# A SwiGLU feed-forward layer: part of the down projection split into two 64-row halves by tile position

## The chip, the core and the metric

The kernel runs on one core of a Trainium2 chip. A core has TensorE (PE in the profile: matrix products, with its weight loads shown apart as PEld), VectorE (DVE), ScalarE (ACT), GpSimd (POOL) and SyncE (SP), which issues transfers. The engines run their own instruction streams and wait for one another by semaphores. TensorE reads its operands from SBUF and writes sums to PSUM, which has eight banks of 512 f32 values per partition; ACT and VectorE read PSUM and write back to SBUF, and DMA moves SBUF to and from device memory. The metric is the device time of one execution in microseconds (us), taken as the median of several runs.

## The reference

```python
B, S, D, F = 1, 2048, 640, 1536        # all bfloat16
def reference(x, w_gate, w_up, w_down):
    g = silu(x @ w_gate)
    u = x @ w_up
    return (g * u) @ w_down
```

`x` is 2048 rows of 640 numbers; the hidden size F is 1536. The two projections up take 2 x 2048 x 640 x 1536 multiplications, the projection down half as many as those two together.

## The kernel before, in words

Everything on chip is kept transposed, with the contracted dimension on the partitions: `xT` (x with D on partitions, KD = 5 blocks of 128), `wg_sb` and `wu_sb` (5 blocks of 128 rows of D), `wd_sb` (KF = 12 blocks of 128 rows of F), and `aT`, the product of silu(gate) and up, with F on the partitions in 12 blocks. The rows of x are worked through in four blocks of 512 (`sb` = 0 to 3).

For each block and each of the 12 chunks of F (`fc`), `proj` (L204) runs five matmuls into a gate bank `pg` and five into an up bank `pu`; `gate` then runs silu on ACT (L221) and the multiplication into `aT` on VectorE (L222). Four PSUM banks (`gu`) rotate here. When a block's 12 chunks are done, the down projection of that block follows, in two parts:

- Columns 512 to 639 of the output, the "column-by-row" part that is edited: twelve matmuls (L287), one for each block `kf` of F, with a 128 x 128 block of `wd_sb` as the weights and 512 columns of `aT` streamed (384 in the last block, whose last 128 rows of x are done otherwise). They accumulate in one bank, `po_t`, from the pool tag `po_b`, which has two banks. The result has output columns on partitions, so it must be turned: ACT copies it to `ot_t` in bf16 (L296), VectorE turns it in squares of 32 (`ot_q`, L298), and ACT's queue issues four stores (L300).
- Columns 0 to 511: for each of the four sub-blocks of 128 rows (`j`), a chain of twelve matmuls (L316) with `aT` as the weights and 512 columns of `wd_sb` streamed, into one of the two banks of tag `po_a`. ACT copies the result (L325) and SP's queue issues the store (L334). The last sub-block of all runs as two chains of 256 columns and one of 128 (the rows that the first part left out), the last one in a bank of tag `po_b` and copied by VectorE (L328).

VectorE has a further task. The last T = 4 rows of x are left out of the `proj` matmuls of the last block, and their gate and up values are computed as dot products on VectorE (`row_dots`, L153, 96 of them, each with a short read of its accumulator). They are dealt out by `do_dots(n)`: two behind most gates, three behind the copy to `ot_t`, three behind each of `j` = 1 to 3. All of them are done before the last block's down projection; `row_tail` (L167, L168) then writes those four columns of `aT`.

The order on VectorE and on SP is the order in which the program is written (`keep_order` ties each instruction of the queue to the one before). On ACT and TensorE the instructions stand in the order written as well. Engines wait only for data and for buffers: a bank of `po_a` is free for chain j + 2 when ACT has copied chain j, and the copies stand on ACT behind the four stores of `ot_q`, which wait for the turning on VectorE.

Of the kernel before, what the change touches and what calls it, by code (L numbers as in the profile page):

```python
# [10 lines left out]
def _body(  # L11
# [8 lines left out]
    nc = tc.nc  # L20
    P = nc.NUM_PARTITIONS
    f32 = mybir.dt.float32
    bf16 = mybir.dt.bfloat16
    ACT = mybir.ActivationFunctionType
    ALU = mybir.AluOpType

    B, S0, D = x.shape
# [6 lines left out]
    KF = F // P  # L34
    S_BLK = 512
    NSB = S // S_BLK
    SUB = S_BLK // P
    DA = 512
# [13 lines left out]
    work = ctx.enter_context(tc.tile_pool(name="work", bufs=3))  # L52
    outp = ctx.enter_context(tc.tile_pool(name="outp", bufs=3))
    psum = ctx.enter_context(
        tc.tile_pool(name="psum", bufs=2, space=bass.MemoryType.PSUM)
    )
# [6 lines left out]
    wd_sb = consts.tile([P, KF, D], bf16)  # L63
    aT = consts.tile([P, KF, S], bf16)
# [45 lines left out]
    def turn_x(c0, c1, k0=0, k1=KD):  # L110
        s_sl = slice(c0 * P, c1 * P)
        nc.sync.dma_start_transpose(out=xT[:, k0:k1, s_sl], in_=xt_v[s_sl, k0:k1])
# [22 lines left out]
    def turn_w(dst, src):  # L135
        for a in range(0, KF, WT_STEP):
            nc.sync.dma_start_transpose(
                out=dst[:, a : a + WT_STEP, :], in_=src[:, a : a + WT_STEP, :]
            )
# [3 lines left out]
        out=x_row[:],  # L143
# [20 lines left out]
    def row_tail():  # L164
        for _ in dots:
            pass
        nc.scalar.activation(row_s[:], row_g[:], ACT.Silu)  # L167
        nc.vector.tensor_tensor(  # L168
            out=aT[:, :, S - T : S], in0=row_s[:], in1=row_u[:], op=ALU.mult
        )  # L170
# [3 lines left out]
    def do_dots(n):  # L174
        for _ in range(n):
            next(dots, None)
# [25 lines left out]
    def proj(ps, w_sb, fc, sb, c0, c1, k0=0, k1=KD):  # L202
        for kd in range(k0, k1):
            nc.tensor.matmul(  # L204
                ps[:, c0:c1],
                lhsT=w_sb[:, kd, fc * P : (fc + 1) * P],
                rhs=xT[:, kd, sb * S_BLK + c0 : sb * S_BLK + c1],
                start=(kd == 0),
                stop=(kd == KD - 1),
            )  # L210

    def gu_tiles():
        pg = psum.tile([P, S_BLK], f32, tag="gu", name="pg", bufs=4)
        pu = psum.tile([P, S_BLK], f32, tag="gu", name="pu", bufs=4)
        return pg, pu

    def gate(pg, pu, sb, fc, n_s):

        s0 = sb * S_BLK
        sg = work.tile([P, S_BLK], f32, name="sg")  # L220
        nc.scalar.activation(sg[:, 0:n_s], pg[:, 0:n_s], ACT.Silu)  # L221
        nc.vector.tensor_tensor(  # L222
            out=aT[:, fc, s0 : s0 + n_s], in0=sg[:, 0:n_s], in1=pu[:, 0:n_s], op=ALU.mult
        )
# [46 lines left out]
    for sb in range(NSB):  # L271
        n_s = S_BLK if sb < NSB - 1 else S_BLK - T
        for fc in range(KF):
            if sb == 0 and fc < N_FIRST:
                continue
            pg, pu = gu_tiles()
            proj(pg, wg_sb, fc, sb, 0, n_s)
            proj(pu, wu_sb, fc, sb, 0, n_s)
            gate(pg, pu, sb, fc, n_s)
            if sb > 0 and fc < KF - 2:  # L280
                do_dots(2)


        n_t = (SUB if sb < NSB - 1 else SUB - 1) * P
        po_t = psum.tile([P, n_t], f32, tag="po_b", name="po_t")
        for kf in range(KF):
            nc.tensor.matmul(  # L287
                po_t[:],
                lhsT=wd_sb[:, kf, DA:D],
                rhs=aT[:, kf, sb * S_BLK : sb * S_BLK + n_t],  # L290
                start=(kf == 0),
                stop=(kf == KF - 1),
            )
        ot_t = outp.tile([P, n_t], bf16, name="ot_t")
        ot_q = outp.tile([P, n_t], bf16, name="ot_q")
        nc.scalar.copy(ot_t[:], po_t[:])  # L296
        do_dots(3)
        nc.vector.transpose(out=ot_q[:], in_=ot_t[:])  # L298
        for q in range(P // Q):
            nc.scalar.dma_start(  # L300
                out=out2[
                    sb * S_BLK : sb * S_BLK + n_t, DA + q * Q : DA + (q + 1) * Q
                ].rearrange("(i r) c -> r i c", r=Q),
                in_=ot_q[q * Q : (q + 1) * Q, :].rearrange("r (i c) -> r i c", c=Q),
            )

        for j in range(SUB):
            s0 = sb * S_BLK + j * P
            last = sb == NSB - 1 and j == SUB - 1
            cols = [(0, DA, "po_a")]  # L310
            if last:
                cols = [(0, DA // 2, "po_a"), (DA // 2, DA, "po_a"), (DA, D, "po_b")]
            for c0, c1, tag in cols:
                po = psum.tile([P, c1 - c0], f32, tag=tag, name="po_a")
                for kf in range(KF):
                    nc.tensor.matmul(  # L316
                        po[:],
                        lhsT=aT[:, kf, s0 : s0 + P],
                        rhs=wd_sb[:, kf, c0:c1],
                        start=(kf == 0),  # L320
                        stop=(kf == KF - 1),
                    )
                ot = outp.tile([P, c1 - c0], bf16, name="ot" if c1 < D else "ot_b")
                if c1 < D:
                    nc.scalar.copy(ot[:], po[:])  # L325
                    eng = nc.sync
                else:
                    nc.vector.tensor_copy(out=ot[:], in_=po[:])  # L328
                    eng = nc.sync
                if 0 < j and not last:  # L330
                    do_dots(3)
                if sb == NSB - 1 and j == ROW_J:
                    row_tail()
                eng.dma_start(out=out2[s0 : s0 + P, c0:c1], in_=ot[:])  # L334
        if sb == 0:
            turn_x(2 * SUB, 3 * SUB)
            turn_w(wuT, wut_v)
            turn_x(3 * SUB, 4 * SUB)
# [72 lines left out]
def kernel(tc, *args):  # L411
    _body(tc, *args)
    tc.close()
    tc.compile()
    _trim(tc.nc)
# [30 lines left out]
```

## Time and profile before

| | |
|---|---|
| Time, median of 3 runs | 163.79 us (163.2 to 163.9) |
| The profiled execution | 163.25 us, of which 161.9 us are the span from the first to the last instruction |
| TensorE busy | 159.6 us, 818 matmuls, granted clock 1.000 |
| VectorE busy | 110.5 us |
| ACT busy | 42.6 us |
| The edited matmuls (L287) | 48, 6% of the chain that ended last |

An instruction is named by its line in the kernel, its engine and operation, and the tiles that it writes and reads (`po_t<-aT,wd_sb`). A group's row gives the count, the busy time in us, the mean duration of one in ns, and the engine's idle time before them with what ended it. In the view by windows of time, a row gives the stretch, its length, and for each engine its busy time in it and the instructions that touch it, then the granted clock and the transfers. A matmul's recorded duration reaches beyond the start of the next one, because matmuls are pipelined, so the pitch from start to start says what one costs in a stream. The chain that ended last lists stretches as start, length, engine and line; the timeline lists start, length and instruction, with the engine's idle time and what ended it in brackets. ACTq stands for transfers that ACT's queue issues.

### The profile page before, as it was taken

What the parts mean: (1) busy time and instruction counts of PE and PEld (TensorE: products, weight loads), DVE (VectorE), ACT (ScalarE), POOL (GpSimd) and SP (SyncE); (2) the same over time, 40 slices, a digit from 0 to 9 for tenths busy, and PEclk for the clock granted to TensorE, in tenths of its full rate; (3) what the DMA queues carried; (4) which work ended last, traced back from release to release, by engine and by line L of the source; (5) the groups of instructions that cost most, each with busy time, mean ns of one, the idle gap of its engine ahead of it and who ended that gap; (6) DMA issues with size and microseconds to landing.
All of it is one profiled execution on the core that took longest, in us unless ns stands there. A gap on an engine that the chain in (4) does not pass through costs nothing.

```text
span 161.9 us, 2159 instructions
## 1 busy us (share of the span) xinstructions
PE 159.6 (99%) x818; PEld 79.9 (49%) x818; DVE 110.5 (68%) x249; ACT 42.6 (26%) x74; POOL 0.6 (0%) x6
## 2 busy tenths in 40 slices
PE   9999999999999999999999999999999999999995
PEld 9885444444444444444444444444444444445454
DVE  1006223599469999989919999979964999993000
ACT  5032222112222222211222322221214222222121
POOL 1000000000000000000000000000000000000000
PEclk9999999999999999999999999999999999999999
DMA  7999999995089992003110000000310000000212
GB/s 228 280 345 348 363 209 241 230 190 100 32 186 139 241 225 58 0 0 34 65 65 4 0 0 2 0 0 4 64 66 32 0 0 0 0 4 0 52 37 73
DMA packets 41209, 15.86 MB, mean 98 GB/s; under 512 B 33264, under 2 KB 41072, under 8 KB 41200
## 3 DMA queue, kind: packets, MB, share of 16 engines
q1 hardware_dynamic: 32832, 14.81, 38.0%
q10 hardware_dynamic: 8368, 0.92, 3.7%
q8 instruction: 6, 0.10, 0.3%
q14 instruction: 3, 0.02, 0.1%
HBM read 6.88 MB, written 2.62 MB: 59 GB/s over the span
## 4 chain that ended last, share of the span: by engine, by line
PE 99%; DVE 0%; issue 0%
PE pu L204 32%; PE pg L204 31%; PE po_a L316 26%; PE po_t L287 6%; PE pg L250 2%; PE pw L182 1%; PE pt L195 1%; DVE ot_b L328 0%; DVE ones L108 0%
## 5 line engine op out<-in xcount | busy, mean ns | idle before, releaser
L204 PE MATMUL pu<-xT,wu_sb 128*128 128x512 bf16 (+2 forms) x260 | 59.3, 362 | 0.0
L204 PE MATMUL pg<-xT,wg_sb 128*128 128x512 bf16 (+2 forms) x240 | 56.9, 370 | 0.0
L222 DVE TENSOR_TENSOR aT<-sg,pu 128x512 bf16<-128x512 f32 (+1 forms) x48 | 32.5, 682 | 32.8 <-PE pu L204 32.8
L221 ACT ACTIVATE sg<-pg 128x512 f32<-128x512 f32 (+1 forms) x48 | 28.4, 597 | 71.1 <-PE pg L204 67.5
L316 PE MATMUL po_a<-wd_sb,aT 128*128 128x512 bf16 (+2 forms) x216 | 42.8, 358 | 0.0
L153 DVE SCALAR_TENSOR_TENSOR prod<-wgT,x_row 128x640 f32<-128x640 bf16 x48 | 39.4, 821 | 1.1
L153 DVE SCALAR_TENSOR_TENSOR prod<-wuT,x_row 128x640 f32<-128x640 bf16 x48 | 39.4, 822 | 1.0
L204 PEld LDWEIGHTS <-wu_sb 128*128 128x128 bf16 x260 | 25.4, 98 | 26.5 <-DMA wu_sb<-in_w_up_dram 0.2
L204 PEld LDWEIGHTS <-wg_sb 128*128 128x128 bf16 x240 | 23.5, 98 | 25.9
L316 PEld LDWEIGHTS <-aT 128*128 128x128 bf16 x216 | 20.7, 98 | 21.6
L325 ACT CAST ot<-po_a 128x512 bf16<-128x512 f32 (+1 forms) x17 | 9.5, 561 | 32.0 <-PE po_a L316 20.9
L287 PE MATMUL po_t<-aT,wd_sb 128*128 128x512 bf16 (+1 forms) x48 | 10.4, 366 | 0.0
L287 PEld LDWEIGHTS <-wd_sb 128*128 128x128 bf16 x48 | 4.7, 98 | 5.1
L328 DVE CAST ot_b<-po_a 128x128 bf16<-128x128 f32 x1 | 0.3, 292 | 9.9 <-PE po_a L316 9.9
L296 ACT CAST ot_t<-po_t 128x512 bf16<-128x512 f32 (+1 forms) x4 | 2.2, 559 | 11.6 <-PE po_t L287 11.6
L153 DVE DVE_READ_ACCUMULATOR prod<-wuT,x_row 128x1 f32 x48 | 4.0, 82 | 0.0
L153 DVE DVE_READ_ACCUMULATOR prod<-wgT,x_row 128x1 f32 x48 | 3.9, 82 | 0.0
L298 DVE STREAM_TRANSPOSE ot_q<-ot_t 128x512 bf16<-128x512 bf16 (+1 forms) x4 | 2.7, 678 | 1.7 <-ACT ot_t L296 1.7
L250 PE MATMUL pg<-xT,wg_sb 128*128 128x256 bf16 (+1 forms) x24 | 3.1, 307 | 0.0
L200 DVE COPY xT<-pt 128x384 bf16<-128x384 bf16 x2 | 0.7, 358 | 3.2 <-PE pt L195 3.2
L250 PEld LDWEIGHTS <-wg_sb 128*128 128x128 bf16 x24 | 2.6, 127 | 0.3
L182 PE MATMUL pw<-ones 128*128 128x128 bf16 x20 | 2.3, 313 | 0.3 <-DVE ones L108 0.3
(15 smaller groups left out, 8.0 us busy)
## 6 DMA issues: line engine op xcount, KB each, us to landing
wd_sb<-in_w_down_dram SPq DMA_DIRECT2D x1, 1920.0 KB, 14.6
out_dram<-ot SPq DMA_DIRECT2D x15, 128.0 KB, 1.7
wg_sb<-in_w_gate_dram SPq DMA_DIRECT2D x2, 640.0 KB, 6.7
wu_sb<-in_w_up_dram SPq DMA_DIRECT2D x2, 640.0 KB, 8.0
x_row<-in_x_dram SPq DMA_DIRECT2D x1, 640.0 KB, 4.9
wg_sb<-in_w_gate_dram SPq DMA_DIRECT2D x3, 128.0 KB, 3.5
wu_sb<-in_w_up_dram SPq DMA_DIRECT2D x1, 384.0 KB, 4.7
out_dram<-ot_q ACTq DMA_DIRECT2D x12, 32.0 KB, 2.1
```

The source lines that it names most:

```text
L153: nc.vector.scalar_tensor_tensor(out=prod[:], in0=wT[:, fc, :], scalar=1.0, in1=x_row[:, t, :], op0=ALU.mult, op1=ALU.mult, accum_out=acc[ ...
L182: nc.tensor.matmul(pw[:, 0:P], lhsT=ones[:].broadcast_to([P, P]), rhs=ones[:].broadcast_to([P, P]), start=True, stop=True,)
L195: nc.tensor.transpose(out=pt[:, kd - k0, :], in_=x_sb[:, c, kd * P : (kd + 1) * P], identity=ident[:],)
L204: nc.tensor.matmul(ps[:, c0:c1], lhsT=w_sb[:, kd, fc * P : (fc + 1) * P], rhs=xT[:, kd, sb * S_BLK + c0 : sb * S_BLK + c1], start=(kd == 0 ...
L221: nc.scalar.activation(sg[:, 0:n_s], pg[:, 0:n_s], ACT.Silu)
L222: nc.vector.tensor_tensor(out=aT[:, fc, s0 : s0 + n_s], in0=sg[:, 0:n_s], in1=pu[:, 0:n_s], op=ALU.mult)
L250: nc.tensor.matmul(pg[:, c0:c1], lhsT=wg_sb[:, kd, wslice(fc, fc + 1)], rhs=xT[:, kd, c0:c1], start=(kd == 0 and c0 == 0), stop=(kd == KD ...
L287: nc.tensor.matmul(po_t[:], lhsT=wd_sb[:, kf, DA:D], rhs=aT[:, kf, sb * S_BLK : sb * S_BLK + n_t], start=(kf == 0), stop=(kf == KF - 1),)
L296: nc.scalar.copy(ot_t[:], po_t[:])
L298: nc.vector.transpose(out=ot_q[:], in_=ot_t[:])
L316: nc.tensor.matmul(po[:], lhsT=aT[:, kf, s0 : s0 + P], rhs=wd_sb[:, kf, c0:c1], start=(kf == 0), stop=(kf == KF - 1),)
L325: nc.scalar.copy(ot[:], po[:])
```

## The change

The twelve matmuls of the column-by-row part become 24. Each block of 128 rows of F is cut in two halves of 64 rows: partitions 0 to 63 of `wd_sb` and `aT` go to the array at row position 0 and accumulate in the first bank, partitions 64 to 127 go to row position 64 and accumulate in a second bank. The two alternate in the program, each with a weight load of its own in front. Both banks have the tag `po_b`, so they are that tag's two buffers. At the end ACT copies the first bank to a new f32 tile `part` in SBUF, and VectorE, behind the three dot products that were there before, adds `part` and the second bank into `ot_t` in bf16. The turning and the stores follow as before. The instructions of all other engines and lines keep their places; in the whole kernel there are 48 more matmuls, 48 more weight loads and four more VectorE instructions.

```diff
         n_t = (SUB if sb < NSB - 1 else SUB - 1) * P
-        po_t = psum.tile([P, n_t], f32, tag="po_b", name="po_t")
+        half = P // 2
+        po_ts = [psum.tile([P, n_t], f32, tag="po_b", name="po_t") for _ in range(2)]
         for kf in range(KF):
-            nc.tensor.matmul(
-                po_t[:],
-                lhsT=wd_sb[:, kf, DA:D],
-                rhs=aT[:, kf, sb * S_BLK : sb * S_BLK + n_t],
-                start=(kf == 0),
-                stop=(kf == KF - 1),
-            )
+            for h, po_t in enumerate(po_ts):
+                h_sl = slice(h * half, (h + 1) * half)
+                nc.tensor.matmul(
+                    po_t[:],
+                    lhsT=wd_sb[h_sl, kf, DA:D],
+                    rhs=aT[h_sl, kf, sb * S_BLK : sb * S_BLK + n_t],
+                    start=(kf == 0),
+                    stop=(kf == KF - 1),
+                    tile_position=(h * half, 0),
+                )
         ot_t = outp.tile([P, n_t], bf16, name="ot_t")
         ot_q = outp.tile([P, n_t], bf16, name="ot_q")
-        nc.scalar.copy(ot_t[:], po_t[:])
+        part = work.tile([P, n_t], f32, name="part")
+        nc.scalar.copy(part[:], po_ts[0][:])
         do_dots(3)
+        nc.vector.tensor_tensor(
+            out=ot_t[:], in0=part[:], in1=po_ts[1][:], op=ALU.add
+        )
         nc.vector.transpose(out=ot_q[:], in_=ot_t[:])
```

## The prediction

> **What bounds the kernel now.** I read the page's busy shares and its chain that ended last first.
>
> ```profile
> PE 159.6 (99%) x818; PEld 79.9 (49%) x818; DVE 110.5 (68%) x249; ACT 42.6 (26%) x74; POOL 0.6 (0%) x6
> PEclk9999999999999999999999999999999999999999
> PE 99%; DVE 0%; issue 0%
> PE pu L204 32%; PE pg L204 31%; PE po_a L316 26%; PE po_t L287 6%; PE pg L250 2%; PE pw L182 1%; PE pt L195 1%; DVE ot_b L328 0%; DVE ones L108 0%
> ```
>
> TensorE (PE) is busy in 99% of the span at the full granted clock, and the chain is TensorE's own instructions from end to end. Whatever lengthens TensorE's stream lengthens the kernel; whatever lengthens another engine costs nothing until a buffer comes free too late for TensorE. The edited line, L287, is 6% of that chain. The chain in order of time shows its four stages and what follows each without a gap:
>
> ```profile
> 30.56 2.59 PE po_t L287 x12
> 33.15 10.36 PE po_a L316 x48
> 69.41 2.59 PE po_t L287 x12
> 72.00 10.36 PE po_a L316 x48
> 108.26 2.59 PE po_t L287 x12
> 110.85 10.36 PE po_a L316 x48
> 146.91 1.95 PE po_t L287 x12
> 148.86 11.07 PE po_a L316 x72
> ```
>
> A 512-column matmul takes 2.59/12 = 0.216 us of the stream, a 384-column one 1.95/12 = 0.162 us: the columns streamed set the pitch. The four stages hold 3 x 2.59 + 1.95 = 9.72 us. The groups with shapes kept apart, and the engines' busy time in two of those stages on that line alone:
>
> ```profile
> L287 PE MATMUL po_t<-aT,wd_sb 128*128 128x512 bf16 x36 | 8.3, 379 | 0.0
> L287 PE MATMUL po_t<-aT,wd_sb 128*128 128x384 bf16 x12 | 2.1, 326 | 0.0
> L287 PEld LDWEIGHTS <-wd_sb 128*128 128x128 bf16 x48 | 4.7, 98 | 5.1
> L316 PE MATMUL po_a<-wd_sb,aT 128*128 128x128 bf16 x12 | 0.8, 219 | 0.0
> ...
> 69.41:72.00 2.59, 2.59 (x12) 0.98 (x10) 1.00 0.00 0
> 146.91:148.86 1.95, 1.95 (x12) 0.97 (x10) 1.00 0.00 0
> ```
>
> One matmul lasts 379 ns but the next follows after 216: 163 ns of each lie under its successor (326 - 162 = 164 for the short ones). Weight loads (98 ns) lie wholly beside the matmuls.
>
> **The change, part by part.** Each of the 48 matmuls over 128 rows of f becomes two over 64 rows, at row positions 0 and 64, each with its own weight load and into its own bank. The columns streamed per instruction stay 512 or 384. So 96 matmuls and 96 loads replace 48 and 48; what decides is whether the two halves stream together.
>
> *A pair of halves.* No row shows two matmuls in the array at once. The bounds are one pitch per pair (216 and 162 ns, nothing added) and two (9.72 us more in all). Nothing in issue forbids the low end, as the end of the chain shows:
>
> ```profile
> 157.94 1.99 PE po_a L316 x24
> 159.93 0.02 issue
> 159.95 0.29 DVE ot_b L328
> ```
>
> These 24 are twelve of 256 columns, at half of 216 ns each, and twelve of 128, which leaves (1.99 - 12 x 0.108)/12 = 0.058 us for a matmul with its load. Two matmuls and two loads thus need some 0.116 us of issue, under 0.162 and 0.216. The halves share no row of the array, no bank and no operand partition. I take one pitch per pair, by reasoning and not by a row, and keep the other end as a rival. The second half's load stands in the program behind the first half's matmul, so that half trails by about 0.058 us and shows once at each stage's end: 4 x 0.058 = 0.23 us, between 0 and 4 x 0.098 = 0.39.
>
> *Entering and leaving the two-half layout.* All other matmuls use the array whole, so each of four stages changes the layout twice, eight changes. No row shows one. At the least it is free, as the step from one line's matmuls to the next is now. At the most the new layout waits until the last matmul is through (163 ns beyond its pitch) and then loads weights in the open (98 ns): 0.261 us. I take 0.163, the wait without the load, since loads run ahead beside matmuls in every row here: 8 x 0.163 = 1.30 us (0 to 2.09).
>
> The Trainium skill, "TensorEngine Tiling (Array Packing)", section Key Properties, says that a change of tiling mode drains TensorE, and that different tiles load and multiply in parallel. By the first the eight waits are there, by the second the pairs are; no row here shows either.
>
> *ACT and VectorE.* ACT's copy of the first bank has the old one's place and, into f32, still 512 columns; the row nearest to it is L221's f32 output, at 597 ns against 586, so nothing. VectorE gets four additions, one per stage, with the operands of L222's form (f32 from SBUF and f32 from PSUM, bf16 out):
>
> ```profile
> L222 DVE TENSOR_TENSOR aT<-sg,pu 128x512 bf16<-128x512 f32 x36 | 24.3, 683 | 28.4 <-PE pu L204 28.4
> L221 ACT ACTIVATE sg<-pg 128x512 f32<-128x512 f32 x36 | 21.3, 597 | 53.6 <-PE pg L204 50.1 <-DVE aT L222 3.5
> L296 ACT CAST ot_t<-po_t 128x512 bf16<-128x512 f32 x3 | 1.8, 586 | 9.2 <-PE po_t L287 9.2
> ```
>
> 0.683 us each, in front of the transpose. Behind that transpose ACT's queue holds the four `ot_q` stores and then the copy of the first `po_a` chain, which frees the bank for the third chain. In order of time (start, length), the second stage, and that copy in the other three:
>
> ```profile
> 72.03 0.59 ACT L296 CAST ot_t<-po_t 128x512 bf16<-128x512 f32 x1 [3.07 <-PE po_t L287]
> 72.65 0.71 DVE L298 STREAM_TRANSPOSE ot_q<-ot_t 128x512 bf16<-128x512 bf16 x1
> 73.39 2.07 ACTq L300 DMA_DIRECT2D out_dram<-ot_q  x4
> 75.51 0.59 ACT L325 CAST ot<-po_a 128x512 bf16<-128x512 f32 x1 [2.89 <-DMA out_dram<-ot_q]
> ...
> 36.58 0.59 ACT L325 CAST ot<-po_a 128x512 bf16<-128x512 f32 x1 [2.81 <-DVE prod L153]
> 114.28 0.59 ACT L325 CAST ot<-po_a 128x512 bf16<-128x512 f32 x1 [2.81 <-DMA out_dram<-ot_q]
> 152.00 0.59 ACT L325 CAST ot<-po_a 128x512 bf16<-128x512 f32 x1 [2.62 <-DMA out_dram<-ot_q]
> ...
> 84.62 0.69 DVE L222 TENSOR_TENSOR aT<-sg,pu 128x512 bf16<-128x512 f32 x1 [3.61 <-PE pu L204]
> ```
>
> In the second stage that copy ends at 76.10. The third chain starts two chains (2 x 2.59) after 72.00, less the 0.16 by which a matmul starts before its predecessor ends: 77.02. Slack 0.92; the other stages, reckoned alike, have 1.00, 1.00 and 1.29. An addition of 0.683 plus a hand-over of some 0.03 (72.03 + 0.59 to 72.65) leaves about 0.2 us at the tightest, more where TensorE itself is later. So I cost it at nothing; without that cover it would be up to 0.7 us in each of three stages. The next gate waits 3.61 us for TensorE on VectorE, so 0.68 more of VectorE's time is hidden there too. The stores behind the addition leave 0.7 us later in mid-kernel; SP's queue is not touched, and the `po_a` stores on it follow ACT's copy. The second bank: both `po_b` buffers are free one stage, some 36 us, before they are wanted, and in the last stage the final 128 columns take the one that ACT released ten us before. After the last matmul nothing is changed.
>
> **Sum.** 0 (pairs) + 0.23 (trail) + 1.30 (changes of layout) + 0 (ACT, VectorE) = +1.53 us, between 0 and 0.39 + 2.09 = 2.48. The profiled execution took 163.25 (span 161.9 and 1.35 around it), so 164.8; it was 0.54 under the median of the three runs, 163.79, and on that scale the forecast is 165.3.
>
> **The rivals.**
> - *Not slower: the change of layout is free.* Then only the trail remains, +0.23, 164.0 on the median's scale. For it: every step from one line to another is seamless in the chain. Against it: none of those steps changes the layout. It decides if a change costs under (0.82 - 0.23)/8 = 0.07 us, 0.82 being 0.5% of 163.79, about what a measurement of this kernel can tell from no change.
> - *The change doesn't do what it says: the halves follow one another.* 36 x 0.216 + 12 x 0.162 = 9.72 more, with the layouts 11.0: 174.8 (173.5 to 175.9). For it: every matmul in the trace starts a full pitch after the one before. Against it: disjoint rows and banks.
> - *A half's weights can't load while that half streams.* Then each pair shows a load that is covered now: 0.058 to 0.098 us x 48 = 2.8 to 4.7, with 1.30 for the layouts +4.1 to +6.0: 167.9 to 169.8. Against it: now all 128 rows stream while the next weights load, 0.98 us of loads inside 2.59 us of matmuls. The Trainium skill, "TensorE: Matmul & The Clock Gate", section Part 3 (packing small matmuls), states that LDWEIGHTS overlaps matmuls in flight only where the row group differs; by that the trace before would show gaps, and it shows none, so the trace disagrees.
> - *ACT's late copy becomes a wait.* If the addition costs double (1.37), three stages wait some 0.4 us, the last one little: about +1.3 on top, 166.6. Against it: the L222 row is the same form, 36 times.
>
> **How the numbers follow.** Pairs together with costly layout changes 0.45; pairs with free changes 0.20; halves one after another 0.20; loads exposed 0.08; ACT's wait 0.04; something faster, for which I see no mechanism, 0.03. The likeliest alone gives 165.3, with its own range 163.8 to 166.3. The other cases but the serial one hold under 0.8, so the range must reach it: 163.4 (a free change within the runs' spread of 163.2 to 163.9) to 174.8. Slower by over 0.5% means over 164.6: the serial, load and ACT cases 0.32 and all but about 0.07 of the likeliest, 0.38, so 0.70. Within 0.5%: the free change and that 0.07, so 0.27. Faster: 0.03.
>
> **What would show it.** In the profile after: L287's successor has 96 matmuls. Right: the four stages take about 2.65, 2.65, 2.65 and 2.01 us plus a wait of about 0.16 at both edges of each, with the second half starting some 0.06 after the first and pairs 0.216 apart. Serial: stages of 5.2 and 3.9. Exposed loads: pairs 0.27 to 0.31 apart. Free change: no gap at the edges. ACT's wait: TensorE idle at the third `po_a` chain, released by ACT. All else on TensorE should stand as it did; what makes the forecast wrong is the pitch of a pair first, and the price of a layout change second.

## The result, and the profile after

The changed kernel takes 164.9 us (median of five runs, 164.64 to 165.76) against 163.79 (five runs, 163.2 to 163.94): a ratio of 1.0093, 95% interval 1.0071 to 1.0115, which is 1.5 us (1.2 to 1.9); the two medians alone differ by 1.1. The profiled execution took 164.64 us with a span of 162.7.

The page of the changed kernel: the busy shares, the two groups of the halves (now L290) and the two new steps, ACT's copy to `part` and VectorE's addition.

```profile
PE 160.4 (99%) x866; PEld 79.1 (49%) x866; DVE 113.2 (70%) x253; ACT 42.6 (26%) x74; POOL 0.6 (0%) x6
...
L290 PE MATMUL po_t<-aT,wd_sb 64*128 64x512 bf16 (+1 forms) x96 | 10.4, 364 | 0.0
L290 PEld LDWEIGHTS <-wd_sb 64*128 64x128 bf16 x96 | 4.4, 94 | 5.9 <-issue 1.7
...
L301 ACT COPY part<-po_t 128x512 f32<-128x512 f32 (+1 forms) x4 | 2.2, 560 | 12.1 <-PE po_t L290 12.1
L303 DVE TENSOR_TENSOR ot_t<-part,po_t 128x512 bf16<-128x512 f32 (+1 forms) x4 | 2.6, 654 | 2.0 <-ACT part L301 1.8
```

96 matmuls in place of 48 keep TensorE busy for the same 10.4 us. The chain that ended last, in order of time, of the changed kernel:

```profile
6.61 2.36 PE pu L204 x20
...
30.60 2.70 PE po_t L290 x24
33.29 5.29 PE po_a L324 x24
39.01 5.18 PE po_a L324 x24
69.66 2.70 PE po_t L290 x24
72.36 5.29 PE po_a L324 x24
78.07 5.18 PE po_a L324 x24
108.72 2.70 PE po_t L290 x24
111.42 5.29 PE po_a L324 x24
117.14 5.18 PE po_a L324 x24
147.59 2.06 PE po_t L290 x24
149.64 11.18 PE po_a L324 x72
160.82 0.02 issue
```

A stage takes 2.70 where it took 2.59 (2.06 for 1.95), and the first 24 `po_a` matmuls behind it 5.29 where 24 pitches are 5.18 (in the last stage 11.18 for 11.07). Each of the eight layout changes thus costs 0.11 us, and behind the first stretch nothing else is longer: 8 x 0.107 = 0.86 us. The whole stream bears that out. The same row of the kernel before:

```profile
6.61 2.31 PE pu L204 x20
```

Both kernels begin the stretch of 20 `pu` matmuls at 6.61; the last matmul ended at 159.93 before and at 160.82 now, 0.89 later, of which 0.05 is that first stretch itself (2.36 for 2.31). Start to start in the trace, from the last `pu` matmul ahead of the first stage to the last matmul of all, TensorE's stream takes 129.52 us before and 130.37 now: 0.85 more.

How the halves start is seen in the view by windows, on L290 alone (length, TensorE's busy time and the instructions that touch the window, the same for weight loads), and in the waits of the weight loads:

```profile
30.52:30.54 0.01, 0.01 (x2) 0.01 (x2) 1.00 0.81 188
```

```profile
PEld L290 <- issue: 1.7, 4, 0.4
PEld L324 <- issue: 1.6, 4, 0.4
```

Within 15 ns of the start of the stage's first instruction, at 30.52, both halves are at work. (The chain counts the stage from 30.60, where the recorded end of the matmul before lies.) The start times in the trace stand 4 ns apart, and pairs follow each other after 216. The weight loads, which had no wait of this kind before, now have eight: four on entering (L290), four on leaving (L324). Such a wait of some 0.42 us counts from the end of the load before, which stands a pitch and more ahead of its time in a steady stream, so it is longer than the 0.107 us that TensorE's stream loses.

One thing in this trace the diff doesn't tell. Between the second and the third `po_a` chain of the first three stages (33.29 + 5.29 = 38.58 to 39.01) two `pg` matmuls of the next block now stand, and three follow behind the fourth chain. The planner, which lays out TensorE's order outside the parts that `keep_order` ties, moved them there. What is said ahead of the prediction, that the instructions of all other lines keep their places, is wrong in this point, and so is that TensorE's instructions all stand in the order written. Experiment 9 takes the move back.

The profiled executions differ by 1.39 us, the spans by 0.89. The other 0.50 lies outside the span, from the first to the last instruction that the trace holds: 163.25 - 161.85 = 1.40 before, 164.64 - 162.74 = 1.90 after. The prediction has no term for that; experiments 5 to 7 go after it.

### The profile page after: what moved, and what is told of

It reads as the page before. It is cut to its first block, busy times and chain, and to the rows that moved or that the text cites. A ratio compares the mean times of both kernels' runs of the same rounds, so it can differ in the third digit from the quotient of the medians.

```text
span 162.7 us, 2263 instructions
## 1 busy us (share of the span) xinstructions
PE 160.4 (99%) x866; PEld 79.1 (49%) x866; DVE 113.2 (70%) x253; ACT 42.6 (26%) x74; POOL 0.6 (0%) x6
## 4 chain that ended last, share of the span: by engine, by line
PE 95%; DMA 3%; SPq 1%; DVE 0%; issue 0%
PE pu L204 32%; PE pg L204 30%; PE po_a L324 26%; PE po_t L290 6%; DMA wu_sb<-in_w_up_dram 3%; SPq L118 1%; SPq L88 0%; DVE ot_b L336 0%
## 5 line engine op out<-in xcount | busy, mean ns | idle before, releaser
L324 PE MATMUL po_a<-wd_sb,aT 128*128 128x512 bf16 (+2 forms) x216 | 43.3, 358 | 0.0
L324 PEld LDWEIGHTS <-aT 128*128 128x128 bf16 x216 | 20.4, 98 | 22.4 <-issue 1.6
L290 PE MATMUL po_t<-aT,wd_sb 64*128 64x512 bf16 (+1 forms) x96 | 10.4, 364 | 0.0
L290 PEld LDWEIGHTS <-wd_sb 64*128 64x128 bf16 x96 | 4.4, 94 | 5.9 <-issue 1.7
L301 ACT COPY part<-po_t 128x512 f32<-128x512 f32 (+1 forms) x4 | 2.2, 560 | 12.1 <-PE po_t L290 12.1
L303 DVE TENSOR_TENSOR ot_t<-part,po_t 128x512 bf16<-128x512 f32 (+1 forms) x4 | 2.6, 654 | 2.0 <-ACT part L301 1.8
```

Of the source, the lines that this page charges most:

```text
L290: nc.tensor.matmul(po_t[:], lhsT=wd_sb[h_sl, kf, DA:D], rhs=aT[h_sl, kf, sb * S_BLK : sb * S_BLK + n_t], start=(kf == 0), stop=(kf == KF - 1),
L301: nc.scalar.copy(part[:], po_ts[0][:])
L303: nc.vector.tensor_tensor(out=ot_t[:], in0=part[:], in1=po_ts[1][:], op=ALU.add)
L324: nc.tensor.matmul(po[:], lhsT=aT[:, kf, s0 : s0 + P], rhs=wd_sb[:, kf, c0:c1], start=(kf == 0), stop=(kf == KF - 1),)
```

## The experiments

All are set against runs of the kernel before on the same chip. "Outside" is a run's time less its span, as a median; for the kernel before it was 1.38 to 1.42 in every group of runs.

**1. The price of a layout change: six times as many of them.** Only the even blocks `kf` are cut in halves.

```diff
         for kf in range(KF):
+            if kf % 2 == 1:
+                nc.tensor.matmul(po_ts[0][:], lhsT=wd_sb[:, kf, DA:D],
+                    rhs=aT[:, kf, sb * S_BLK : sb * S_BLK + n_t],
+                    start=False, stop=(kf == KF - 1))
+                continue
             for h, po_t in enumerate(po_ts):
...
-                    stop=(kf == KF - 1),
+                    stop=(h == 1 and kf == KF - 2),
```

> The changed kernel with only every other block kf cut in halves; the odd blocks run as whole matmuls into the first bank. Twelve layout changes per stage in place of two, 48 in place of 8. Theory (each change costs about 0.107 us): +5.1 us over before, 168.9; 4.3 over the changed kernel. Rival (a change costs only where a stage begins or ends, with its change of operands and banks, or the remaining 0.4 us are a cost of the pairs): 164.4 to 165.0.

Measured: 168.58 us, ratio 1.0318 (1.030 to 1.0336), 5.2 us over the 163.39 of the kernel before; 5.2/48 = 0.108 for a change. The chain of this kernel (L299 the halves, L289 the whole ones) and the loads' waits:

```profile
30.87 0.32 PE po_t L299 x2
31.19 0.32 PE po_t L289
31.52 0.32 PE po_t L299 x2
31.84 0.32 PE po_t L289
```

```profile
PEld L299 <- issue: 6.0, 24, 0.4
PEld L289 <- issue: 5.1, 24, 0.2
```

Every step between layouts is 0.32 us where the pitch is 0.216, 24 waits in and 24 out. The price is that of a change of layout as such, not of a stage's beginning.

**2. and 3. Fewer of them.** The change in the first stage only, and in the first three. The diff of the first; the other has `sb < NSB - 1`.

```diff
+        if sb == 0:
             po_ts = [psum.tile(...) for _ in range(2)]
...
+        else:
+            po_t = psum.tile([P, n_t], f32, tag="po_b", name="po_t")
...
+            nc.scalar.copy(ot_t[:], po_t[:])
```

> The change in the first of the four stages only; the other three as in the kernel before. Two layout changes in place of eight. Theory (0.107 us for each): 0.21 in TensorE's stream, span 0.2 longer than that of the kernel before. Rival (the cost is one for the whole kernel, not one for each change): 0.86 in the stream. The time outside the span: 1.7 if one addition brings it, 1.4 if not.

> The change in the first three stages; the last one as in the kernel before, so six layout changes. Theory (0.107 us for each): TensorE's stream 0.64 longer, 0.21 less than in the changed kernel. For the time outside the span: 1.75 and more in all kernels with the addition in four stages and whole or halved matmuls, 1.4 with the addition in the first stage only and in the kernels without it. If the last stage's addition (near the end of the kernel) brings it: 1.4, and 0.65 over the kernel before; if the number of additions does: 1.75, and 1.0 over.

Measured: 163.98 against 163.56, ratio 1.0026 (1.0011 to 1.0041), outside 1.38; and 164.2 against 163.44, ratio 1.0054 (1.0035 to 1.0073), outside 1.61. The loads' waits, of the kernel with one stage and of that with three:

```profile
PEld L291 <- issue: 0.4, 1, 0.4
PEld L339 <- issue: 0.4, 1, 0.4
```

```profile
PEld L339 <- issue: 1.3, 3, 0.4
PEld L291 <- issue: 1.3, 3, 0.4
```

Two waits and six. The first stage of the one reads 2.70, its other three 2.59 and 1.95: 0.21 of the 0.42 us (0.2 to 0.7) is in the stream, as the theory has it, and the interval reaches down to it. The other 0.2 lies in the span (162.6 against 162.2 by the medians) but not in the stages: in the profiled execution the last `pu` matmul ahead of the first stage starts at 30.83 where it started at 30.18 before, so the kernel's head differed, and no run says why. The three give 0.64 in the stream and 0.2 outside, 0.84 of the 0.88. One addition alone brings no time outside. Neither of the two answers offered for the time outside fits 1.61.

**4. Do the halves pair by themselves?** The loops swapped: twelve matmuls of the first half, then twelve of the second.

```diff
-        for kf in range(KF):
-            for h, po_t in enumerate(po_ts):
+        for h, po_t in enumerate(po_ts):
+            for kf in range(KF):
```

> The changed kernel with the loops swapped: all twelve matmuls of the first half, then all twelve of the second, so that neighbours in TensorE's stream use the same 64 rows. Theory (two matmuls stream together only when their row positions differ and they are neighbours in the stream): the stages double, 9.72 us more, 174.0 to 174.9, stages of 5.3 and 4.0 us. Rival (TensorE looks ahead over the stream and pairs the halves by itself, or a matmul of 64 rows costs half): as the changed kernel, 164.6 to 165.5.

Measured: 171.42 us, ratio 1.0469 (1.040 to 1.054), 7.7 us more. Both were off. The stages in this kernel's chain:

```profile
31.14 4.44 PE po_t L290 x24
...
71.95 4.44 PE po_t L290 x24
...
112.75 4.44 PE po_t L290 x24
...
153.36 3.37 PE po_t L290 x24
```

24 matmuls one after another would take 24 x 0.216 + 0.11 = 5.29. The stage is 0.85 shorter, about four pitches. Start to start, the trace shows single matmuls at 216 ns, then, with the ninth of the first half, a second one 8 ns behind it, and pairs from there until the first half is through. So TensorE started the second half's first matmul with three matmuls of the first half still in front of it in the program: matmuls of different row positions pair by neighbourhood, but over a reach of some three matmuls, not only for direct neighbours. All four stages show the same. The planner might have mixed the two lists itself; the semaphore marks in the trace speak against it. As in the kernel before, where the twelve stand alone, the tenth matmul of the first half raises TensorE's semaphore for those ahead of it, the eleventh and twelfth raise it by one each, and no matmul of the second half counts among them. A run with TensorE's order tied was not made. Two on the same 64 rows keep the full pitch, so half the rows is not half the time.

**5. The path without the halves.** Whole matmuls, the blocks alternating between two banks, with `part` and the addition.

```diff
-            for h, po_t in enumerate(po_ts):
-                h_sl = slice(h * half, (h + 1) * half)
...
+            nc.tensor.matmul(
+                po_ts[kf % 2][:],
+                lhsT=wd_sb[:, kf, DA:D],
+                rhs=aT[:, kf, sb * S_BLK : sb * S_BLK + n_t],
+                start=(kf < 2), stop=(kf >= KF - 2))
```

> The array is used whole again (12 matmuls of 128 rows per stage), but the blocks kf alternate between the two banks, and the copy to part and VectorE's addition stay. No layout change is left. Theory (the cost is eight layout changes of about 0.107 us, 0.86 us, ACT and VectorE are hidden): the time of the kernel before, 163.8 within 0.3, span 161.9. Rival (the longer path over part and the addition costs something, in the stream or behind the span): 164.3 to 164.6, the part of the 1.1 to 1.5 us that 0.86 doesn't explain.

Measured: 163.91 against 163.39, ratio 1.0026 (1.001 to 1.0042). The chain of this kernel:

```profile
69.44 2.59 PE po_t L288 x12
72.03 5.18 PE po_a L321 x24
77.21 0.43 PE pg L204 x2
77.64 5.18 PE po_a L321 x24
```

TensorE's stream is that of the kernel before to 0.01 us, so the copy, the addition and the later stores are hidden in it. But all twelve runs have 1.70 to 1.80 outside (median 1.75) against 1.38: against the kernel before on the same chip the theory's "nothing" fell by some 0.4 us, nearly all of it outside the span. That 163.91 still lies within its 163.8 +- 0.3 is chance: on this chip the kernel before took 163.39 and not 163.79.

**6. The halves without the path.** The second bank is never read.

```diff
-        part = work.tile([P, n_t], f32, name="part")
-        nc.scalar.copy(part[:], po_ts[0][:])
+        nc.scalar.copy(ot_t[:], po_ts[0][:])
         do_dots(3)
-        nc.vector.tensor_tensor(
-            out=ot_t[:], in0=part[:], in1=po_ts[1][:], op=ALU.add)
```

> The changed kernel without the second half's way out: ACT copies the first bank to ot_t in bf16 as before, and part and VectorE's addition are gone (the second half's sum is left out of the output; TensorE does all of its work). Theory (0.86 us of layout changes in the stream; the rest of the difference, 0.3 to 0.7 us, lies outside the span and goes with the addition's path): 0.9 over the kernel before, span 162.8, time outside the span 1.4 as in the kernel before. Rival (the rest goes with TensorE's matmuls by halves): 1.5 over, time outside the span 1.7 or more.

Measured: 164.64 against 163.61, ratio 1.0074 (1.0041 to 1.0107), 1.2 us (0.7 to 1.8), which holds the theory's 0.9 and the rival's 1.5; span 163.2 against 162.2 (medians); outside 1.42, with nine of twelve runs between 1.37 and 1.44 and three between 2.0 and 2.6. The stages are 2.70 and 2.06 again. The median outside is that of the kernel before, as the theory has it, but three of the twelve runs have more without any addition.

**7. What else could bring the time outside.** Three kernels: VectorE gets a tiny instruction in the addition's place; the path goes over `part`, but from one bank; and experiment 5 with a slightly longer program for TensorE.

```diff
         do_dots(3)
+        nc.vector.memset(tiny[:], 1.0)
```

> The kernel before with one tiny VectorE instruction per stage (a memset of one column, read by nobody) where the changed kernel has its addition, so four VectorE instructions more and nothing else. In the kernel with whole matmuls and the addition the stream and the span were those of before, but the time outside the span was 1.74 us against 1.38. Theory A (the time outside the span goes with the program's code, not with the work): 1.7 outside, 0.35 over the kernel before. Theory B (it goes with the path over part and the addition): 1.4 outside, no difference.

```diff
-        nc.scalar.copy(ot_t[:], po_t[:])
+        part = work.tile([P, n_t], f32, name="part")
+        nc.scalar.copy(part[:], po_t[:])
         do_dots(3)
+        nc.vector.tensor_copy(out=ot_t[:], in_=part[:])
```

> The kernel before, one bank and whole matmuls, but ACT copies the bank to part in f32 and VectorE copies part to ot_t in bf16 behind the dot products: the changed kernel's longer path without the second bank. Kernels with the addition had 1.7 us and more outside the span in four of five cases, those without it 1.4. Theory (the path, a later start of the transpose and the stores, brings it): time outside the span 1.7, 0.4 over the kernel before. Rival (it goes with the place of the program's code or with the second bank): 1.4 outside, no difference.

```diff
-    N_WARM = 20
+    N_WARM = 24
```

> The kernel with whole matmuls in two banks and the addition, with 24 in place of 20 warming matmuls at the start, so that TensorE's program is eight instructions longer and the rest the same. Theory (the time outside the span goes with the addition's path): 1.75 outside as without the four, the span longer by up to 0.4. Rival (it goes with where the program's code lies, which the four shift): another value, 1.4 or 2.1.

Measured: 163.42 against 163.61, ratio 0.9994 (0.9977 to 1.001), outside 1.42; 163.66 against 163.56, ratio 1.0008 (0.9994 to 1.0021), outside 1.39; 164.06 against 163.56, ratio 1.0031 (1.0019 to 1.0043), outside 1.76. So neither four more VectorE instructions nor the longer path from one bank brings it, and eight more instructions for TensorE don't move it. The kernels that add two banks have it: 1.75, 1.76, 1.77 (experiment 4), 1.61 with three additions, 1.94 and 2.07 in the two groups of runs of the changed kernel, 2.04 in experiment 9. Three things contradict: experiment 1 has all four additions and 1.39 outside, one addition alone gives 1.38, and three runs of experiment 6 have 2.0 to 2.6 without one. The trace holds nothing before the first and behind the last instruction, and behind the last matmul these kernels' traces are equally long (1.92 to 1.94 us, with the addition and without). What this time is stays open.

**8. More instructions without a layout change.** The matmuls of the kernel before, cut by columns.

```diff
+            for c0 in (0, n_t // 2):
+                s0 = sb * S_BLK + c0
                 nc.tensor.matmul(
-                    po_t[:],
+                    po_t[:, c0 : c0 + n_t // 2],
                     lhsT=wd_sb[:, kf, DA:D],
-                    rhs=aT[:, kf, sb * S_BLK : sb * S_BLK + n_t],
+                    rhs=aT[:, kf, s0 : s0 + n_t // 2],
```

> The kernel before with each of the 48 po_t matmuls cut into two of half the columns (256, or 192 in the last stage), whole array, one bank, no addition: as many TensorE instructions as in the changed kernel, no layout change. Theory: two halves of the columns cost one whole one, some 2 ns more each from the 109 against 108 ns pitch: +0.1 us, 163.9. Rival (48 more matmuls and weight loads cost something in themselves, by loading of code or by issue): 164.3 to 164.9.

Measured: 163.74 against 163.39, ratio 1.0021 (1.0001 to 1.0041), outside 1.42. The chain of this kernel:

```profile
30.53 2.62 PE po_t L289 x24
```

0.03 more for twelve matmuls and twelve loads more in a stage, 0.12 in all four. It is not the number of instructions that makes 2.70 out of 2.59, and the interval, 0.02 to 0.67 us, leaves the rival (0.5 to 1.1 over the 163.79 it was reckoned from) only its lower end.

**9. The moved `pg` matmuls put back.**

```diff
     keep_order(mybir.EngineType.SP)
+    keep_order(mybir.EngineType.PE)
```

> The changed kernel with TensorE's instructions held in the order of the program, so that the two pg matmuls which now stand between the second and third po_a chain go back behind the fourth. Theory (their place costs nothing; the third chain would still find its bank free about 0.3 us before it starts): the time of the changed kernel, 164.9 within 0.3, no idle TensorE at the third chain. Rival (the addition makes ACT's copy late, and the moved matmuls hide it): TensorE idle at the third chain released by ACT, 0.1 to 0.4 us in each of three stages, 165.2 to 166.1.

Measured: 165.1 us, ratio 1.0106 (1.0088 to 1.0124), which overlaps the changed kernel's interval. The chain of this kernel, and ACT's copies in its second stage:

```profile
70.16 2.70 PE po_t L290 x24
72.85 10.47 PE po_a L324 x48
```

```profile
74.97 2.09 ACTq L308 DMA_DIRECT2D out_dram<-ot_q  x4
77.10 0.59 ACT L333 CAST ot<-po_a 128x512 bf16<-128x512 f32 x1 [3.62 <-DMA out_dram<-ot_q]
```

The 48 matmuls take 10.47 where they took 10.36 before, the 0.11 of the layout change and no idle time. The third chain begins at 72.85 + 5.29 - 0.16 = 77.98, and the copy that frees its bank ends at 77.69: 0.29 us to spare, the least of the four stages, and what the theory said. TensorE's stream is the changed kernel's 130.37 us, so the place of the `pg` matmuls costs nothing and hides nothing.

**10. The changed kernel again.**

> The changed kernel itself once more, on the same chip as the others. Both theories: 1.0 to 1.6 us over the kernel before, 0.8 to 0.9 of it in TensorE's stream at the eight layout changes; the time outside the span 1.7 or more against 1.4 says how much of it the span doesn't hold.

Measured: 165.33 against 163.61, ratio 1.010 (1.006 to 1.0139); span 163.25 against 162.2, outside 2.07 (1.71 to 2.58). Stages and edges read as in the first trace. TensorE's stream, measured as for the result, takes 130.37 us here and in experiment 6 too; it takes 129.52 in the three kernels of experiment 7 and in experiment 5, as in the kernel before, 129.73 with two layout changes, 130.16 with six and 134.63 with 48. That is 0.106 to 0.107 us a change in every case.

## Why the prediction was right, and where it was not

- *What bounds the kernel.* Right: what TensorE's stream gained the span gained, and 2.7 us more of VectorE's time (110.5 to 113.2) cost nothing in it.
- *A pair of halves at one pitch.* Right: 24 in 2.70 us with the entry. The choice rested on reasoning and no row; experiment 4 shows the other end of that bound for halves out of reach of each other, and so that the alternation in the program matters.
- *The trail of 0.058 us per stage, 0.23 in all.* Wrong: 4 ns a stage, which the cost of leaving already holds. The step took the pitch of a load with a short matmul for the distance of two that may start together; loads and matmuls of the two halves start side by side.
- *The layout change at 0.163 us.* The mechanism was right, the size not: 0.107. The term of 1.30 is 0.86. The next layout doesn't wait until the last matmul's recorded end: its loads start at 30.52, 0.07 ahead of that end (30.60), and its matmuls with them. The reason for leaving the load out, that loads run ahead, doesn't hold at a change either: all eight loads wait. But the matmul starts 4 ns behind its load. So from the last matmul's start to the first of the halves a pitch of 0.216 became 0.311, and the next one is 0.227: 0.095 and 0.011 more, together 0.106.
- *ACT and VectorE at nothing.* Right in the stream: the addition took 0.686, the slack at the third chain was forecast at 0.2 us at the tightest and is 0.29 with the order kept. But some 0.5 us came in outside the span (0.50 in the profiled execution, 0.67 by the medians of the second group of runs), and 0.2 to 0.7 in six of the eight kernels that add two banks. The sum had carried over the 1.35 around the span unchanged: that step failed, and why is not settled.
- *All else on TensorE stays.* Wrong, without a price: the planner moved two `pg` matmuls in each of the first three stages.
- *The sum.* +1.53 forecast, 1.5 (1.2 to 1.9) by the ratio, 1.1 by the medians (164.9 for the 165.3 forecast). Two errors meet in it: 0.67 too much in the stream (0.44 on the layouts, 0.23 on the trail), about 0.5 left out beside it. That the total came out so near is in part luck; by its terms the forecast was less right.
- *The rivals.* Free changes: out, by the eight waits. Halves one after another: out for the program as written. ACT's late copy as a wait: out, TensorE has no idle time at the third chain. A half's weights not loading while it streams: out, since pairs stand 216 ns apart with both next loads between them. The rule in the Trainium skill, "TensorE: Matmul & The Clock Gate", Part 3, that LDWEIGHTS overlaps only where the row group differs thus doesn't hold in this trace either. The statement in the Trainium skill, "TensorEngine Tiling (Array Packing)", Key Properties, that a change of mode drains TensorE, agrees with the eight waits, at 0.107 us a change.

## What to carry to other kernels

Cutting a full 128-row contraction in two 64-row halves gains nothing on TensorE here, as two halves together take the pitch of one whole matmul. Whether it pays where rows would stand idle was not run. Where row positions are used, alternate them in the program (in experiment 4 the separate lists cost up to 1.74 us a stage) and gather all work of one layout in one stretch, since each way in or out cost about 0.11 us. Set the profiled time against the span when a small difference is explained: here a third of it (0.50 of 1.39 us) lay outside the span, where no view of the trace reaches.

## What was not expected of the hardware

By the starts in its trace and the semaphore marks, TensorE in experiment 4 started matmuls of the other row position ahead of their place in the program, with three others still in front, which saved about four pitches (0.85 us) of a stage of 5.29. And on a change of layout weight load and first matmul start within 4 ns of each other; the next matmul on those rows follows after 227 ns in place of 216, so by the recorded starts a load that isn't made ahead cost about 0.015 us of the 0.107.
